# TensorE's batches 8 to 31 as a hardware loop, with fixed K and V slots, in a cached grouped-query attention block

## The chip, the cores and the metric

The kernel runs on one core of a Trainium2 chip. The metric is the device time of one execution in microseconds (us). The kernel before takes 367.31 us, the median of three runs that lie between 367.27 and 367.34.

The profile's span is about 2 us shorter than the time (365.4 against 367.2 us for the profiled run of before). Spans and stamps within a trace count from the first instruction.

## The reference, cut to what matters

```python
B, Sq, D = 32, 4, 1024
Hq, Hkv, Sk, Dh = 32, 4, 2048, 128
q = (x @ wq).reshape(B, Sq, Hq, Dh).transpose(0, 2, 1, 3)
k = jnp.repeat(k_cache, rep, axis=1)          # rep = Hq // Hkv = 8
v = jnp.repeat(v_cache, rep, axis=1)
p = softmax(einsum("bhqd,bhkd->bhqk", q, k) * Dh ** -0.5)
o = einsum("bhqk,bhkd->bhqd", p, v)
return o.transpose(0, 2, 1, 3).reshape(B, Sq, Hq * Dh) @ wo     # all bf16
```

The K and V of one batch are 2 MB each. With 32 batches and 8 MB each of wq and wo, the core must read 151 MB. That makes this a problem of keeping the DMA full (its load queue is busy 98.0% of the span, table below).

## The kernel before: the parts that matter here

Each engine has its own instruction list, written out for all 32 batches. A batch goes through these steps: VectorE transposes K (`kt`, four chunks), TensorE computes the scores (QK), VectorE the maximum, ScalarE the exponential, VectorE transposes P (`pt`), POOL spreads it into a block-diagonal operand (`pd`), TensorE multiplies by V (PV), and a small product turns O around (OT). At the end the output product uses wo.

K, V, wq and wo go through eight SBUF slots of 2 MB, used as a ring in load order. All loads are issued by SyncE (SP) in program order, and each waits until the last user of its slot is done:

```python
for n, (kind, b) in enumerate(loads):
    s = ring_slot(n)
    before, holder[s], slot_of[kind, b] = holder.get(s), (kind, b), s
    waits = [] if before is None else ["qproj"] if before == "w" else [
        ("kt", before[1], NCH - 1) if before[0] == "k" else ("pv", before[1])]
    ...
    p.dma("sp", lambda e, s=s, src=src: e.dma_start(big[:, s, :, :], src), waits, (kind, b), f"s_b{s}")
```

Every instruction that somebody waits for increments the one semaphore of its engine, and a wait compares with an absolute count:

```python
def op(self, engine, emit, waits=(), done=None):
    ...
    if done is not None:
        self.count[engine] += 1
        self.at[done] = (engine, self.count[engine])
```

From batch 9 on, one of the eight slots becomes the second buffer of the spread P (`PF_sb`); until then there are eight slots for loads.

Of the kernel before, what the change touches and what calls it, by code (L numbers as in the profile page):

```python
# [29 lines left out]
class _Program:  # L30
# [6 lines left out]
    def __init__(self):  # L37
        self.ops = {e: [] for e in self.ENGINES}
        self.count = {e: 0 for e in self.ENGINES}
        self.at = {}  # L40
        self.dma_count = {}
        self.last_pool = None

    def op(self, engine, emit, waits=(), done=None):
        if engine == "pool":
            done = done or ("pool", self.count["pool"])
            waits = tuple(waits) + (self.last_pool,) * (self.last_pool is not None)
            self.last_pool = done
        if done is not None:
            assert done not in self.at, done  # L50
            self.count[engine] += 1
            self.at[done] = (engine, self.count[engine])
        self.ops[engine].append((emit, tuple(waits), done is not None, None))

    def dma(self, engine, emit, waits, done, sem):
        assert done not in self.at, done
        self.dma_count[sem] = self.dma_count.get(sem, 0) + 16
        self.at[done] = (sem, self.dma_count[sem])
        self.ops[engine].append((emit, tuple(waits), False, sem))

    def emit(self, name, engine, sems):
        seen = {}
        for emit, waits, counted, dma_sem in self.ops[name]:
            need = {}
            for w in waits:
                s, n = self.at[w]
                if seen.get(s, 0) < n:
                    need[s] = max(need.get(s, 0), n)
            for s, n in need.items():
                engine.wait_ge(sems[s], n)  # L70
                seen[s] = n
            ins = emit(engine)
            if counted:
                ins.then_inc(sems[name], 1)
            if dma_sem is not None:
                ins.then_inc(sems[dma_sem], 16)


def bass_standalone__gqa_block_cached__sampling_kernel(
# [23 lines left out]
    SL = 17  # L103
    SW = 12
    SPB = 9
# [8 lines left out]
    with ExitStack() as es:  # L114
# [42 lines left out]
        for c in range(4):  # L157
            p.dma("sp", lambda e, c=c: e.dma_start(w_sb[:, 2 * c:2 * c + 2, :], wq_v[:, 2 * c:2 * c + 2, :]),  # L158
                  [], ("wq", c), f"s_b{c}")

        loads = [("k", b) for b in range(LEAD)]
        for b in range(B):
            ahead = [b + LEAD] if b < SL else [b + LEAD, b + LEAD + 1] if b == SL else [b + LEAD + 1]
            loads += [("k", a) for a in ahead if a < B] + [("v", b)]
        n_pd = loads.index(("k", SPB + LEAD))
        spare = (NW + n_pd) % NS
        pd_holder = loads[n_pd - NS]

        def ring_slot(n):
            if n < n_pd:  # L170
                return (NW + n) % NS
            return (spare + 1 + (n - n_pd) % (NS - 1)) % NS

        PF_sb = big[:, spare, :, :].rearrange("p t d -> p (t d)").rearrange("p (t g q w) -> p t g q w", t=T // 2, g=G, q=32)
        slot_of = {}
        holder = {s: "w" for s in range(NW)}
        for n, (kind, b) in enumerate(loads):
            s = ring_slot(n)
            before, holder[s], slot_of[kind, b] = holder.get(s), (kind, b), s
            waits = [] if before is None else ["qproj"] if before == "w" else [  # L180
                ("kt", before[1], NCH - 1) if before[0] == "k" else ("pv", before[1])]
            src = (k_cache if kind == "k" else v_cache)[b].rearrange("g (r t) d -> (g r) t d", r=R)
            p.dma("sp", lambda e, s=s, src=src: e.dma_start(big[:, s, :, :], src), waits, (kind, b), f"s_b{s}")
        n = len(loads)
        wo_slot = [ring_slot(n + c) for c in range(NW)]
# [6 lines left out]
        for c, m in enumerate(WO):  # L192
            assert h0 // 8 == (h0 + m - 1) // 8
            kind, b = holder[wo_slot[h0 // 8]]
# [17 lines left out]
        p.op("pool", lambda e: e.memset(words(PD_sb[:, :, :, :, :].rearrange("p t g q w -> p (t g q w)")), 0.0), [], "pd0")  # L212

# [47 lines left out]
        freed = [("qe", m, 1) for m in range(4)]  # L261

        def slot(free):
            n = len(freed)
            freed.append(free)
            return ring[n % 4], [freed[n - 4]]
# [4 lines left out]
        def qd(i):  # L271
            for g in range(G):
# [5 lines left out]
                     ("qd", i) if g == G - 1 else None)  # L278

        def kt(i, chunks):  # L280
            for c in chunks:
                ts = slice(TC * c, TC * (c + 1))
                src = words(big[:, slot_of["k", i], ts, :].rearrange("p t d -> p (t d)"))
                dst = words(KT_sb[:, i % 2, ts, :, :, :].rearrange("p t a r w -> p (t a r w)"))
                waits = [("k", i)] + ([("qk", i - 2)] if i > 1 else ["qt_all"] if i == 1 else [])
                p.op("dve", lambda e, s=src, d=dst: e.transpose(d, s), waits, ("kt", i, c))  # L286

        def pe_qk(i):
            waits = [("kt", i, NCH - 1), ("qd", i)] + ([("exp", i - 1)] if i else [("qs", j) for j in range(8)])
            for a in range(2):  # L290
                for w in range(2):
                    for c in range(NCH):
# [10 lines left out]
                        p.op("pe", mm, waits, ("qk", i) if last and c == NCH - 1 else None)  # L303
# [6 lines left out]
        def softmax_exp(i):  # L310
# [3 lines left out]
                [("negmx", i)] + ([("pt", i - 1)] if i else ["qproj"]), ("exp", i))  # L314

# [6 lines left out]
        def pd_of(i):  # L322
            return PF_sb if i > SPB and i % 2 else PD_sb

        def pd(i):
            free = [j for j in range(i) if pd_of(j) is pd_of(i)]
            free = ("pv", free[-1]) if free else "pd0" if pd_of(i) is PD_sb else "pf0"
            for g in range(G):
# [3 lines left out]
                p.op("pool", lambda e, s=src, d=dst: e.tensor_copy(d, s), [("pt", i), free], ("pd", i, g))  # L332

        def pe_pv(i, t):
            if t == 0:
                ring_of["o", i], waits = slot(("o", i))
# [154 lines left out]
```

## Time and profile before

| what | value |
|---|---|
| time | 367.31 us (367.27 to 367.34) |
| DMA queue 1 | busy 98.0%, 421 to 434 GB/s in slices 2 to 37 |
| TensorE / VectorE busy | 78% / 74% |
| one batch in the chain of waits | 8.92 us |
| K and V of one batch on the DMA | 2 x 4.89 us = 9.79 us |

Parts 1 to 3 of the profile page of before show busy time by engine, then the span in 40 equal slices (a digit is the busy share in tenths), then the DMA queues with packets, MB and share. In all views PE is TensorE's products, PEld its weight loads, DVE VectorE, ACT ScalarE, POOL GpSimd, and SPq the load issues of SyncE:

```profile
span 365.4 us, 6102 instructions
...
PE 285.7 (78%) x2837; PEld 140.1 (38%) x2368; DVE 271.7 (74%) x270; ACT 107.6 (29%) x135; POOL 166.9 (46%) x265
...
PEclk9998668999999999998889999999999999989999
DMA  8999999999999999999999999999999999999993
GB/s 328 430 425 429 434 429 421 430 429 428 428 429 425 427 427 426 427 430 425 430 427 427 425 424 424 421 430 429 430 429 425 427 425 423 429 423 423 406 402 120
...
q1 hardware_dynamic: 12416, 151.39, 98.0%
q8 instruction: 20, 0.33, 0.4%
```

The DMA row is full from end to end, so, apart from the 4.2 us between the last landing and the end, the kernel can only end earlier if the DMA ends earlier. Queue 8 looks negligible at 0.4%. It is not. The page lists its 20 packets as instructions; they are 16 KB each and about 1.05 us long (0.93 to 1.10). I take them for TensorE's program; at 5,261 TensorE instructions there are 20. The next table shows what they do.

Each load has 16 landings in the trace (1,296 for 81 transfers), which I read as one for each of the 16 DMA engines. The wait for a load ended with the last of them: the wo piece that closes the chain below lands from 353.84 to 358.65 us, and its wait ended at 358.65. I computed this table from the trace's landing records. For the load that lands n-th after the first piece of wq, I subtract n x 4.894 us and give the first and the last of its 16 landings.

```
kernel before       first   last
n=10   (57 us)       0.03   0.34
n=12   (67 us)       0.03   1.61
n=16   (86 us)       0.00   1.66
n=24  (126 us)      -0.01   1.79
n=67  (336 us)      -0.02   4.78
last wo piece       356.46 us / 361.19 us
```

The least disturbed engine keeps its pace to within 0.1 us for 336 us. The most disturbed one falls back in three steps of about 1.3 us (0.3 to 1.6, 1.8 to 3.1, 3.4 to 4.7), after the 1st, 9th and 17th packet of queue 8, which start at 61.6, 191.5 and 308.7 us; it ends at 4.8 us. That every eighth packet met the same engine is read from these steps: the trace does not number the engines.

The end of the chain of waits of before (start, duration, what) shows that the last wo pieces close the kernel:

```profile
295.96 25.15 DMA big<-in_v_cache_dram
...
340.31 18.34 DMA big<-in_wo_dram
```

### The profile page before, as it was taken

To read this page: it belongs to the slowest core of one execution; us is meant where nothing else is said; L and a number is where in the kernel's file an instruction comes from. 1 tells how busy PE (TensorE), PEld (TensorE's weight loads), DVE (VectorE), ACT (ScalarE), POOL (GpSimd) and SP (SyncE) were. 2 spreads that over 40 slices of the span, in tenths; PEclk is the share of its full clock that TensorE was granted. 3 is DMA by queue.
4 is the path that set the end of the run, shared out by engine and by line. 5 is a ranking of instruction groups with operands and counts; after the bars stand their busy time and mean duration, and the time that the engine had idled before them with its cause. 6 is when DMAs were issued, how large, how long until landed. Compare 5 with 4: busy or idle time off the path is not lost.

```text
span 365.4 us, 6102 instructions
## 1 busy us (share of the span) xinstructions
PE 285.7 (78%) x2837; PEld 140.1 (38%) x2368; DVE 271.7 (74%) x270; ACT 107.6 (29%) x135; POOL 166.9 (46%) x265
## 2 busy tenths in 40 slices
PE   1972666888888888877778888888888886889896
PEld 1002001444444444432234444444444443458821
DVE  0029577999999999997788999999999999854000
ACT  1010112333333373332333333333333333334100
POOL 5002150555555555753554555555555555436400
PEclk9998668999999999998889999999999999989999
DMA  8999999999999999999999999999999999999993
GB/s 328 430 425 429 434 429 421 430 429 428 428 429 425 427 427 426 427 430 425 430 427 427 425 424 424 421 430 429 430 429 425 427 425 423 429 423 423 406 402 120
DMA packets 12586, 151.90 MB, mean 416 GB/s; under 512 B 1296, under 2 KB 1552, under 8 KB 3856
## 3 DMA queue, kind: packets, MB, share of 16 engines
q1 hardware_dynamic: 12416, 151.39, 98.0%
q8 instruction: 20, 0.33, 0.4%
q10 hardware_dynamic: 144, 0.13, 0.1%
q14 instruction: 6, 0.05, 0.0%
HBM read 151.26 MB, written 0.26 MB: 415 GB/s over the span
## 4 chain that ended last, share of the span: by engine, by line
PE 37%; DVE 22%; ACT 19%; DMA 18%; issue 2%; POOL 2%; SPq 0%; POOLq 0%
PE ps_s L16 24%; ACT P_sb L311 18%; DVE mx L306 17%; PE ps_s L298 9%; DMA big<-in_v_cache_dram 7%; DMA big<-in_wq_dram 6%; DMA big<-in_wo_dram 5%; PE ps_r L341 4%; DVE KT_sb L286 2%; POOL PD_sb L332 2%; DVE negmx L307 1%; DVE QT_sb L258 1%; DVE KT_sb L242 1%; PE ps_s L374 0%; SPq L158 0%
## 5 line engine op out<-in xcount | busy, mean ns | idle before, releaser
L286 DVE STREAM_TRANSPOSE KT_sb<-big 128x1024 f32<-128x1024 f32 x128 | 150.5, 1216 | 0.8 <-DMA big<-in_k_cache_dram 0.8
L332 POOL COPY PD_sb<-PT_sb 32x1024 f32<-32x1024 f32 x84 | 86.9, 1035 | 92.0 <-PE ps_r L341 69.8
L16 PE MATMUL ps_s<-KT_sb,QD_sb 128*128 128x512 bf16 x384 | 112.3, 402 | 0.0
L311 ACT ACTIVATE P_sb<-ps_s,negmx 128x2048 bf16<-128x2048 f32 x32 | 81.4, 2545 | 96.7 <-DVE negmx L307 96.7
L298 PE MATMUL ps_s<-KT_sb,QD_sb 128*128 128x512 bf16 x128 | 51.6, 403 | 59.0 <-ACT P_sb L311 50.6
L306 DVE TENSOR_REDUCE mx<-ps_s 128x1 f32<-128x2048 f32 x32 | 73.3, 2292 | 23.5 <-PE ps_s L16 23.5
L341 PE MATMUL ps_r<-big,PD_sb 128*128 128x128 bf16 x1344 | 79.0, 219 | 2.9 <-DMA big<-in_v_cache_dram 2.2
L341 PEld LDWEIGHTS ps_r<-big,PD_sb 128*128 128x128 bf16 x1344 | 75.3, 98 | 5.7 <-DMA big<-in_v_cache_dram 2.3
L298 PEld LDWEIGHTS ps_s<-KT_sb,QD_sb 128*128 128x128 bf16 x128 | 13.0, 102 | 143.7 <-issue 78.2
L332 POOL COPY big<-PT_sb 32x1024 f32<-32x1024 f32 x44 | 45.5, 1035 | 41.0 <-PE ps_r L341 38.6
L319 DVE STREAM_TRANSPOSE PT_sb<-P_sb 128x1024 f32<-128x1024 f32 x32 | 39.9, 1245 | 14.4 <-ACT P_sb L311 14.4
L277 POOL COPY QD_sb<-QT_sb 32x64 f32<-32x64 f32 x128 | 29.5, 230 | 41.7 <-DVE QT_sb L258 25.5
L341 PE MATMUL ps_r<-big 128*128 128x128 bf16 x704 | 42.8, 223 | 3.0 <-DMA big<-in_v_cache_dram 2.4
L364 ACT ACTIVATE oT_sb<-ps_r 128x128 bf16<-128x128 f32 x32 | 8.9, 278 | 116.1 <-PE ps_r L359 116.1
L341 PEld LDWEIGHTS ps_r<-big 128*128 128x128 bf16 x704 | 40.9, 100 | 3.6 <-DMA big<-in_v_cache_dram 2.7
L382 DVE CAST P_sb<-ps_s 128x512 bf16<-128x512 f32 x1 | 0.7, 692 | 25.8 <-PE ps_s L374 25.8
L359 PEld LDWEIGHTS ps_r<-ident,o_sb 128*64 128x64 bf16 x128 | 4.6, 109 | 31.2 <-issue 29.0
L242 DVE CAST KT_sb<-ps_r 128x512 bf16<-128x512 f32 x2 | 1.3, 687 | 19.9 <-PE ps_r L226 19.9
L16 PE MATMUL ps_s<-big,oT_sb 128*128 128x512 bf16 x32 | 12.1, 379 | 0.7 <-ACT oT_sb L364 0.7
L348 ACT ACTIVATE o_sb<-ps_r,rinv 128x128 bf16<-128x128 f32 x32 | 11.2, 350 | 3.7 <-PE ps_r L341 3.7
L374 PE MATMUL ps_s<-big,oT_sb 128*128 128x512 bf16 x30 | 11.4, 379 | 0.2 <-DMA big<-in_wo_dram 0.2
L16 PE MATMUL ps_s<-big,P_sb 128*128 128x512 bf16 x32 | 9.1, 411 | 0.0
(29 smaller groups left out, 60.8 us busy)
## 6 DMA issues: line engine op xcount, KB each, us to landing
big<-in_k_cache_dram SPq DMA_DIRECT2D x32, 2048.0 KB, 21.7
big<-in_v_cache_dram SPq DMA_DIRECT2D x32, 2048.0 KB, 20.4
big<-in_wq_dram SPq DMA_DIRECT2D x4, 2048.0 KB, 13.9
big<-in_wo_dram SPq DMA_DIRECT2D x7, 1024.0 KB, 27.2
big<-in_wo_dram SPq DMA_DIRECT2D x1, 512.0 KB, 17.2
big<-in_wo_dram SPq DMA_DIRECT2D x2, 256.0 KB, 14.9
P_sb<-in_x_dram SPq DMA_DIRECT2D x1, 256.0 KB, 2.9
out_dram<-P_sb SPq DMA_DIRECT2D x1, 128.0 KB, 1.8
```

Source lines behind the costliest of these rows:

```text
L16: return eng.add_instruction(mybir.InstMatmult(name=nc.get_next_instruction_name(), engine=eng.engine, start_tensor_calc=start, stop_tenso ...
L277: p.op("pool", lambda e, s=src, d=dst: e.tensor_copy(d, s), waits if g == 0 else [], ("qd", i) if g == G - 1 else None)
L286: p.op("dve", lambda e, s=src, d=dst: e.transpose(d, s), waits, ("kt", i, c))
L298: mm = lambda e, a_=(out_, lhsT, rhs), f=first, l=last: e.matmul(a_[0], lhsT=a_[1], rhs=a_[2], start=f, stop=l, skip_group_check=True)
L306: p.op("dve", lambda e: e.tensor_reduce(mx[:, i % 4:i % 4 + 1], ps_s[:, :], AX.X, ALU.max), [("qk", i)], ("mx", i))
L311: p.op("act", lambda e: e.activation(P_sb[:, :, :, :].rearrange("p t r w -> p t w r"), ps_s[:, :].rearrange("p (t w r) -> p t w r", w=2, r=R),
L319: p.op("dve", lambda e: e.transpose(dst, src), [("exp", i)] + ([("pd", i - 2, G - 1)] if i > 1 else []), ("pt", i))
L332: p.op("pool", lambda e, s=src, d=dst: e.tensor_copy(d, s), [("pt", i), free], ("pd", i, g))
L341: p.op("pe", lambda e: e.matmul(buf[:, 0:Dh], lhsT=pd_of(i)[:, t // 2, :, :, t % 2].rearrange("p g q -> p (g q)"), rhs=big[:, slot_of["v", ...
L348: p.op("act", lambda e: e.activation(o_sb[:, :], buf[:, 0:Dh], ACT.Copy, scale=rinv[:, i % 4:i % 4 + 1]), [("pv", i), ("rinv", i)] + ([("o ...
L364: p.op("act", lambda e: e.activation(oT_sb[:, :, :, i * Sq:(i + 1) * Sq].rearrange("p h e s -> p e h s"), buf[:, 0:128].rearrange("p (e h ...
L374: mm = lambda e, a=(out_, lhsT, rhs), h=h: e.matmul(a[0], lhsT=a[1], rhs=a[2], start=(h == 0), stop=(h == Hq - 1), skip_group_check=True)
```

## The change

The intent is that TensorE's program shrinks from 5,261 instructions to 2,228, because batches 8 to 31 run as six turns of a loop over four batches. The body is written once, with the same wait values and addresses in all six turns. An absolute count, which grows from turn to turn, does not fit it, so TensorE's waits become tokens that are counted down when taken. For the addresses, V has four fixed slots (b mod 4), K has three (b mod 3), and the eighth slot is the second P buffer from the start. Idle products (4 of 512 columns per batch) are added between QK and PV from batch 4 on, with four more after PV in batches 4 to 7. PV falls back by one batch over batches 4 to 7, in the kernel before over 12 to 15. VectorE takes five of the eight copies of the last two P spreads. The order of the load queue is retuned.

The core of the diff, with cuts marked:

```diff
+    def op(self, engine, emit, waits=(), done=None, takes=(), gives=None):
+        ...
+        if gives is not None:
+            self.late[engine].append(done)
+        elif done is not None:
             self.count[engine] += 1
-            self.at[done] = (engine, self.count[engine])
+            for d in [done] + self.late[engine]:
+                self.at[d] = (engine, self.count[engine])
+            self.late[engine] = []
 ...
+        run(ops[:marks[0]])
+        with engine.Fori(0, len(parts)):
+            run(parts[0])
+        run(ops[marks[-1]:])
 ...
+            loads += [("v", b)] + ks if b < S1 else ks + [("v", b)]
+
+        def slot_of(kind, b):
+            return b % VS if kind == "v" else VS + b % KS        # VS = 4, KS = 3
 ...
-                p.op("dve", lambda e, s=src, d=dst: e.transpose(d, s), waits, ("kt", i, c))
+                p.op("dve", lambda e, s=src, d=dst: e.transpose(d, s), waits, ("kt", i, c), gives="t_kt" if c == NCH - 1 else None)
 ...
-            waits = [("kt", i, NCH - 1), ("qd", i)] + ([("exp", i - 1)] if i else [...])
+            takes = [("t_kt", 1), ("t_qd", 1)] + [("t_exp", 1)] * (i > 0)
 ...
-            return PF_sb if i > SPB and i % 2 else PD_sb
+            return PF_sb if i % 2 else PD_sb
 ...
-                p.op("pool", ..., ("pd", i, g))
+                p.op("dve" if i >= B - 2 and g < i - B + 4 else "pool", ..., ("pd", i, g))
 ...
+            if SW <= i < B:
+                pe_idle(4)
 ...
+        p.loop = starts[SW + EASE:B + 1:4]
```

In this program an instruction increments one semaphore.

More of the change, by code (lines that the diff above doesn't have):

```diff
@@ L40, in __init__ @@
         self.at = {}
+        self.late = {e: [] for e in self.ENGINES}
         self.dma_count = {}
         self.last_pool = None
-    def op(self, engine, emit, waits=(), done=None):
+        self.loop = None
+    def op(self, engine, emit, waits=(), done=None, takes=(), gives=None):
         if engine == "pool":
@@ L48, in op @@
             self.last_pool = done
-        if done is not None:
-            assert done not in self.at, done
+        if gives is not None:
+            self.late[engine].append(done)
+        elif done is not None:
             self.count[engine] += 1
-            self.at[done] = (engine, self.count[engine])
-        self.ops[engine].append((emit, tuple(waits), done is not None, None))
-    def dma(self, engine, emit, waits, done, sem):
+            for d in [done] + self.late[engine]:
+                assert d not in self.at, d
+                self.at[d] = (engine, self.count[engine])
+            self.late[engine] = []
@@ L56, in dma, with give @@
+        self.ops[engine].append((emit, tuple(waits), tuple(takes), (gives or engine, 1) if done is not None else None))
+    def give(self, engine, after, gives):
+        self.ops[engine].append((None, (after,), (), (gives, 1)))
+    def dma(self, engine, emit, waits, done, sem, taken=False):
         assert done not in self.at, done
         self.dma_count[sem] = self.dma_count.get(sem, 0) + 16
-        self.at[done] = (sem, self.dma_count[sem])
-        self.ops[engine].append((emit, tuple(waits), False, sem))
+        if not taken:
+            self.at[done] = (sem, self.dma_count[sem])
+        self.ops[engine].append((emit, tuple(waits), (), (sem, 16)))
@@ L61, in emit, with run @@
     def emit(self, name, engine, sems):
         seen = {}
-        for emit, waits, counted, dma_sem in self.ops[name]:
-            need = {}
-            for w in waits:
-                s, n = self.at[w]
-                if seen.get(s, 0) < n:
-                    need[s] = max(need.get(s, 0), n)
-            for s, n in need.items():
-                engine.wait_ge(sems[s], n)
-                seen[s] = n
-            ins = emit(engine)
-            if counted:
-                ins.then_inc(sems[name], 1)
-            if dma_sem is not None:
-                ins.then_inc(sems[dma_sem], 16)
+        def run(ops):
+            for emit, waits, takes, gives in ops:
+                need = {}
+                for w in waits:
+                    s, n = self.at[w]
+                    if seen.get(s, 0) < n or emit is None:
+                        need[s] = max(need.get(s, 0), n)
+                for s, n in need.items():
+                    ins = engine.wait_ge(sems[s], n)
+                    seen[s] = n
+                for s, n in takes:
+                    engine.wait_ge(sems[s], n).then_inc(sems[s], -n)
+                if emit is not None:
+                    ins = emit(engine)
+                if gives is not None:
+                    ins.then_inc(sems[gives[0]], gives[1])
@@ L79, in bass_standalone__gqa_block_cached__sampling_kernel @@
+        ops = self.ops[name]
+        if name != "pe":
+            return run(ops)
+        marks = self.loop
+        parts = [ops[a:b] for a, b in zip(marks, marks[1:])]
+        for part in parts:
+            assert [o[1:] for o in part] == [o[1:] for o in parts[0]] and not any(o[1] for o in part)
+        run(ops[:marks[0]])
+        with engine.Fori(0, len(parts)):
+            run(parts[0])
+        run(ops[marks[-1]:])
 def bass_standalone__gqa_block_cached__sampling_kernel(
@@ L102, in bass_standalone__gqa_block_cached__sampling_kernel @@
     LEAD = 3
-    SL = 17
-    SW = 12
-    SPB = 9
+    S1 = 12
+    S2 = 18
+    VS = 4
+    KS = 3
+    SW = 4
     EASE = 4
@@ L158, in bass_standalone__gqa_block_cached__sampling_kernel @@
             p.dma("sp", lambda e, c=c: e.dma_start(w_sb[:, 2 * c:2 * c + 2, :], wq_v[:, 2 * c:2 * c + 2, :]),
-                  [], ("wq", c), f"s_b{c}")
+                  [], ("wq", c), f"s_w{c}")
         loads = [("k", b) for b in range(LEAD)]
         for b in range(B):
-            ahead = [b + LEAD] if b < SL else [b + LEAD, b + LEAD + 1] if b == SL else [b + LEAD + 1]
-            loads += [("k", a) for a in ahead if a < B] + [("v", b)]
-        n_pd = loads.index(("k", SPB + LEAD))
-        spare = (NW + n_pd) % NS
@@ L167, in bass_standalone__gqa_block_cached__sampling_kernel @@
-        pd_holder = loads[n_pd - NS]
-        def ring_slot(n):
-            if n < n_pd:
-                return (NW + n) % NS
-            return (spare + 1 + (n - n_pd) % (NS - 1)) % NS
-        PF_sb = big[:, spare, :, :].rearrange("p t d -> p (t d)").rearrange("p (t g q w) -> p t g q w", t=T // 2, g=G, q=32)
-        slot_of = {}
-        holder = {s: "w" for s in range(NW)}
-        for n, (kind, b) in enumerate(loads):
-            s = ring_slot(n)
-            before, holder[s], slot_of[kind, b] = holder.get(s), (kind, b), s
-            waits = [] if before is None else ["qproj"] if before == "w" else [
-                ("kt", before[1], NCH - 1) if before[0] == "k" else ("pv", before[1])]
+            ahead = b + LEAD + (b >= S2)
@@ new lines, in bass_standalone__gqa_block_cached__sampling_kernel @@
+            ks = [("k", a) for a in range(len(loads) - b, ahead + 1) if a < B]
+            loads += [("v", b)] + ks if b < S1 else ks + [("v", b)]
+        def slot_of(kind, b):
+            return b % VS if kind == "v" else VS + b % KS
+        PF_sb = big[:, NS - 1, :, :].rearrange("p t d -> p (t d)").rearrange("p (t g q w) -> p t g q w", t=T // 2, g=G, q=32)
+        for kind, b in loads:
+            s = slot_of(kind, b)
+            waits = ["qproj"] * (b < VS) if kind == "v" else []
+            if kind == "v" and b >= VS:
+                waits = [("pv", b - VS)]
+            if kind == "k" and b >= KS:
+                waits = [("kt", b - KS, NCH - 1)]
@@ L182, in bass_standalone__gqa_block_cached__sampling_kernel @@
             src = (k_cache if kind == "k" else v_cache)[b].rearrange("g (r t) d -> (g r) t d", r=R)
-            p.dma("sp", lambda e, s=s, src=src: e.dma_start(big[:, s, :, :], src), waits, (kind, b), f"s_b{s}")
-        n = len(loads)
-        wo_slot = [ring_slot(n + c) for c in range(NW)]
+            p.dma("sp", lambda e, s=s, src=src: e.dma_start(big[:, s, :, :], src), waits, (kind, b), f"s_b{s}", kind == "v")
+        wo_for = [("k", B - 3), ("k", B - 2), ("k", B - 1), ("v", B - 4)]
+        wo_slot = [slot_of(kind, b) for kind, b in wo_for]
@@ L193, in bass_standalone__gqa_block_cached__sampling_kernel @@
             assert h0 // 8 == (h0 + m - 1) // 8
-            kind, b = holder[wo_slot[h0 // 8]]
+            kind, b = wo_for[h0 // 8]
             if m > 1:
@@ L212, in bass_standalone__gqa_block_cached__sampling_kernel @@
         p.op("pool", lambda e: e.memset(words(PD_sb[:, :, :, :, :].rearrange("p t g q w -> p (t g q w)")), 0.0), [], "pd0")
+        p.op("pool", lambda e: e.memset(words(PF_sb.rearrange("p t g q w -> p (t g q w)")), 0.0), [], "pf0")
         for kt in range(KT):
@@ L258, in bass_standalone__gqa_block_cached__sampling_kernel, with slot @@
                 p.op("dve", lambda e, s=src, d=dst: e.tensor_copy(d, s), [("qt", m)], ("qe", m, a))
-        freed = [("qe", m, 1) for m in range(4)]
-        def slot(free):
-            n = len(freed)
-            freed.append(free)
-            return ring[n % 4], [freed[n - 4]]
+        used = []
+        def slot():
+            used.append(len(used))
+            return ring[used[-1] % 4]
         ring_of = {}
@@ L278, in qd @@
                      ("qd", i) if g == G - 1 else None)
+            p.give("pool", ("qd", i), "t_qd")
         def kt(i, chunks):
@@ L282, in kt @@
                 ts = slice(TC * c, TC * (c + 1))
-                src = words(big[:, slot_of["k", i], ts, :].rearrange("p t d -> p (t d)"))
+                src = words(big[:, slot_of("k", i), ts, :].rearrange("p t d -> p (t d)"))
                 dst = words(KT_sb[:, i % 2, ts, :, :, :].rearrange("p t a r w -> p (t a r w)"))
                 waits = [("k", i)] + ([("qk", i - 2)] if i > 1 else ["qt_all"] if i == 1 else [])
-                p.op("dve", lambda e, s=src, d=dst: e.transpose(d, s), waits, ("kt", i, c))
+                p.op("dve", lambda e, s=src, d=dst: e.transpose(d, s), waits, ("kt", i, c), gives="t_kt" if c == NCH - 1 else None)
         def pe_qk(i):
-            waits = [("kt", i, NCH - 1), ("qd", i)] + ([("exp", i - 1)] if i else [("qs", j) for j in range(8)])
+            waits = [] if i else [("qs", j) for j in range(8)]
+            takes = [("t_kt", 1), ("t_qd", 1)] + [("t_exp", 1)] * (i > 0)
             for a in range(2):
@@ L302, in pe_qk @@
                                 nc, e, *a_, tile_size=(128, 128), tile_position=(0, 0), start=f, stop=l)
-                        p.op("pe", mm, waits, ("qk", i) if last and c == NCH - 1 else None)
+                        p.op("pe", mm, waits, ("qk", i) if last and c == NCH - 1 else None, takes)
+                        waits, takes = [], []
         def softmax_max(i):
@@ L314, in softmax_exp @@
                 [("negmx", i)] + ([("pt", i - 1)] if i else ["qproj"]), ("exp", i))
+            if i < L:
+                p.give("act", ("exp", i), "t_exp")
         def pt(i):
@@ L322, in pd_of @@
         def pd_of(i):
-            return PF_sb if i > SPB and i % 2 else PD_sb
+            return PF_sb if i % 2 else PD_sb
         def pd(i):
-            free = [j for j in range(i) if pd_of(j) is pd_of(i)]
-            free = ("pv", free[-1]) if free else "pd0" if pd_of(i) is PD_sb else "pf0"
+            free = ("pv", i - 2) if i > 1 else ("pd0", "pf0")[i]
             for g in range(G):
@@ L331, in pd @@
                 dst = words(pd_of(i)[rows, :, g, :, :].rearrange("p t q w -> p t (q w)"))
-                p.op("pool", lambda e, s=src, d=dst: e.tensor_copy(d, s), [("pt", i), free], ("pd", i, g))
+                p.op("dve" if i >= B - 2 and g < i - B + 4 else "pool", lambda e, s=src, d=dst: e.tensor_copy(d, s), [("pt", i), free], ("pd", i, g))
+            if i < B - 2:
+                p.give("pool", ("pd", i, G - 1), "t_pd")
         def pe_pv(i, t):
+            takes, waits = [], []
             if t == 0:
-                ring_of["o", i], waits = slot(("o", i))
-                waits = waits + [("pd", i, g) for g in range(G)] + [("v", i)]
-            else:
-                waits = []
+                ring_of["o", i] = slot()
+                takes = [("t_pd", 1)] * (i < B - 2) + [(f"s_b{slot_of('v', i)}", 16)]
+                waits = [] if i < B - 2 else [("pd", i, g) for g in range(G)]
             buf = ring_of["o", i]
@@ L342, in pe_pv, with pe_idle @@
                 buf[:, 0:Dh], lhsT=pd_of(i)[:, t // 2, :, :, t % 2].rearrange("p g q -> p (g q)"),
-                rhs=big[:, slot_of["v", i], t, :], start=(t == 0), stop=(t == T - 1)),
-                waits, ("pv", i) if t == T - 1 else None)
+                rhs=big[:, slot_of("v", i), t, :], start=(t == 0), stop=(t == T - 1)),
+                waits, ("pv", i) if t == T - 1 else None, takes)
+        def pe_idle(n):
+            out_, lhsT = ring[len(used) % 4], ident[:, :]
+            rhs = QT_sb[:, 0:4, :, :, :, :].rearrange("p b a h s w -> p (b a h s w)")
+            for c in range(n):
+                if c == 0:
+                    mm = lambda e: e.matmul(out_, lhsT=lhsT, rhs=rhs, start=True, stop=True, skip_group_check=True)
+                else:
+                    mm = lambda e: _matmul_held(nc, e, out_, lhsT, rhs, tile_size=(128, 128), tile_position=(0, 0), start=True, stop=True)
+                p.op("pe", mm)
         def o_evac(i):
@@ L348, in o_evac @@
             p.op("act", lambda e: e.activation(o_sb[:, :], buf[:, 0:Dh], ACT.Copy, scale=rinv[:, i % 4:i % 4 + 1]),
-                 [("pv", i), ("rinv", i)] + ([("oT", i - 1)] if i else []), ("o", i))
+                 [("pv", i), ("rinv", i)] + ([("oT", i - 1)] if i else []), ("o", i), gives="t_o")
         def pe_ot(i):
-            buf, waits = slot(("ot", i))
-            ring_of["ot", i] = buf
+            buf = ring_of["ot", i] = slot()
             for e_ in range(2):
@@ L359, in pe_ot @@
                     p.op("pe", lambda e, a=(out_, lhsT, rhs): e.matmul(a[0], lhsT=a[1], rhs=a[2], start=True, stop=True),
-                         waits + [("o", i)] if e_ == u == 0 else [], ("oT", i) if e_ == u == 1 else None)
+                         [], ("oT", i) if e_ == u == 1 else None, [("t_o", 1)] if e_ == u == 0 else [])
         def ot_evac(i):
@@ L378, in oproj @@
                             nc, e, *a, tile_size=(128, 128), tile_position=(0, 0), start=(h == 0), stop=(h == Hq - 1))
-                    p.op("pe", mm, [("wo", c), ("ot", B - 1), ("exp", B - 1)], ("op", j) if h == Hq - 1 else None)
+                    p.op("pe", mm, [("wo", c), ("ot", B - 1)], ("op", j) if h == Hq - 1 else None)
         def oproj_out():
@@ L391, in pv_until @@
             less = min(max(i - SW + 1, 0), EASE) * (T // EASE)
-            return max((i - 1) * T - less, 0)
+            return max((i - 1) * T - less, 0) if i < B else (i - 2) * T
         qd(0)
@@ L396, in bass_standalone__gqa_block_cached__sampling_kernel @@
         done = 0
-        for i in range(B + 2):
-            upto = pv_until(i) if i < B else (i - 2) * T if i == B else B * T
+        starts = []
+        for i in range(B + 3):
+            starts.append(len(p.ops["pe"]))
+            upto = pv_until(i)
             if i < L:
@@ L405, in bass_standalone__gqa_block_cached__sampling_kernel @@
             j = done // T - 1
-            if i < B and j >= 0 and j not in ot_done:
+            if j >= 0 and j not in ot_done:
                 ot_done.append(j)
-                pe_ot(j)
-                ot_evac(j)
+                if i < B:
+                    pe_ot(j)
+                    ot_evac(j)
+            if SW <= i < B:
+                pe_idle(4)
             if i < B:
                 softmax_exp(i)
-            if i == SPB:
-                p.op("act", lambda e: e.memzero(words(PF_sb.rearrange("p t g q w -> p (t g q w)"))),
-                     [("kt", pd_holder[1], NCH - 1) if pd_holder[0] == "k" else ("pv", pd_holder[1])], "pf0")
             if i < L:
@@ L421, in bass_standalone__gqa_block_cached__sampling_kernel @@
                 if k % T == T - 1:
-                    if i >= B and k // T - 1 not in ot_done:
-                        ot_done.append(k // T - 1)
+                    if i >= B:
                         pe_ot(k // T - 1)
@@ L426, in bass_standalone__gqa_block_cached__sampling_kernel @@
                     o_evac(k // T)
+            if SW <= i < SW + EASE:
+                pe_idle(4)
             done = upto
@@ L434, in bass_standalone__gqa_block_cached__sampling_kernel @@
         oproj_out()
-        names = list(p.ENGINES) + sorted({s for s in p.dma_count})
+        p.loop = starts[SW + EASE:B + 1:4]
+        names = list(p.ENGINES) + ["t_kt", "t_qd", "t_exp", "t_pd", "t_o"] + sorted({s for s in p.dma_count})
         sems = {n: es.enter_context(nc.semaphore(f"e_{n}" if n in p.ENGINES else n)) for n in names}
```

## The prediction

> **What bounds the kernel now.** DMA, throughout. The page gives DMA as 9 tenths in nearly every slice at 425 to 430 GB/s; 2 MB loads land 4.89 us apart from 8 to 336 us. No engine is as full (PE 78%, DVE 74%). In the chain of waits a batch's own cycle (QK, max, exp) repeats every 8.92 us, against 2 x 4.89 = 9.79 us for its K and V: TensorE has 0.87 us to spare per batch.
>
> **The 16 DMA engines.** In the trace's landing records a load's first and last sixteenth are 0.3 us apart until 61 us; then the spread steps to 1.6, at 192 us to 3.1, at 307 us to 4.7, and the last wo piece has its first sixteenth at 356.46 us, its last at 361.19. Each step (about 1.3 us) follows a packet of the instruction queue: 20 packets on queue 8, 16 KB each, about 1.05 us long, some 15 us apart; every eighth hits the same engine again. [...] So fetches cost the last load up to 4.5 us.
>
> **What the change does.**
> - The loop cuts TensorE's code from 5,261 to 1,034 + 670 + 524 instructions. If the 670-instruction body is kept over its six turns, 8 or 9 fetches remain, one or two per affected engine instead of three. I estimate a last spread of 1.8 to 3.1 us: 1.7 to 3.0 us gained, all at the end of the chain (wo).
> - If the body is fetched anew each turn, 20 to 25 fetches and six stalls, nothing gained. [...] A stall under 3.5 us a turn (4 x 0.87) would hide.
> - Idle products: 4 x 0.216 = 0.9 us per batch, inside TensorE's 5.3 us wait for max and exp (beside 3.75 us PV, 0.25 us O). They should prevent half-clock stretches (seven records at 0.5), which cost nothing while DMA is full.
> - [...]
> - Tail: now PV(27) waits for V until 321.1 us, then QK, max, exp, PD(30) and PD(31) on POOL (4.3 us each), PV(31); the output product runs 348.2 to 362.0 us, TensorE-bound at 0.43 us per head, just as wo lands. VectorE taking five of eight quarters frees 2 to 4 us, so the tail can follow the earlier wo. Without this the loop would gain little.
> - Load order and fixed slots: loads stay an estimated 4 to 5 us ahead of an empty queue at the start; neutral.
>
> **Sum.** Last wo near 358.5 us, then 0.4 + 0.7 + 2.8 us for products, eviction, store: span 362.2, time 364.6 us (-0.7%), range 362.6 to 368.0. Faster by over 2% (below 360) is out of reach: even the least disturbed DMA engine ends at 356.5 us. Chances: faster 0.02, same 0.93, slower 0.05.
>
> **What would show it.** Right: 8 or 9 packets on queue 8, none between first and last turn; last wo spread under 3.2 us; loads 4.89 us apart; PEclk 9 from 100 us on; the output product waiting for wo. Wrong: 20 or more packets on queue 8; holes in PE every four batches; gaps in the DMA row; a cycle over 9.8 us.
>
> **What would make it wrong.** A jump that refetches and stalls over 3.5 us; loads held behind a fixed slot so that DMA runs dry; the tail's TensorE path staying the longer one.

The 8 or 9 packets can be worked out from the trace of before: 2,228 x 20 / 5,261 = 8.5. That the body is kept over its turns, or else fetched anew with a stall at each, were two assumptions that no run had shown yet; the 2 to 4 us of the tail are my estimate.

## The result, and the profile after

In its first four runs the changed kernel took 367.24 us median (366.77 to 368.25), against 367.32 us (367.27 to 367.43) for the kernel before, run beside it. The ratio is 1.0001, 95% interval 0.9978 to 1.0024: no difference. Six further runs (the control below) gave 366.17 us median, ratio 0.9986 (0.9965 to 1.0007). Ratios here are the mean time of one kernel's fast runs over that of the other's from the same rounds, so not quite the ratio of the medians quoted. The changed kernel also spreads over more than 2 us, where the kernel before stays within a few tenths.

The same parts of the page of after:

```profile
span 364.8 us, 6484 instructions
...
PE 303.4 (83%) x2942; PEld 142.8 (39%) x2400; DVE 276.6 (76%) x275; ACT 107.6 (30%) x134; POOL 165.7 (45%) x261
...
PEclk9998668999999999999999999999999999999999
DMA  8999999999999999999999999999999999999993
GB/s 334 431 431 426 428 424 401 415 418 425 429 431 426 429 422 428 425 429 428 428 429 430 429 427 429 426 426 431 426 428 431 428 431 427 431 428 420 402 409 140
...
q1 hardware_dynamic: 12416, 151.39, 98.3%
q8 instruction: 8, 0.13, 0.1%
```

The loop does what was hoped: 8 instruction packets instead of 20, none between 140.1 and 335.0 us by their start times in the trace. The QK of batch 12, with which the second turn begins, starts at 149.4 us, so the body of 670 instructions ran its last five turns without a packet. The clock is full from 62 us to the end. The expected 2.7 us did not arrive, and the GB/s row shows where to look: slices 7 to 9 (55 to 82 us) read 401, 415 and 418, where before has 421, 430 and 429.

The chain of waits of after closes with the same load, 0.7 us earlier:

```profile
339.68 18.30 DMA big<-in_wo_dram
```

The landing table of after:

```
kernel after        first   last
n=10   (57 us)       0.02   0.59
n=12   (67 us, K5)   0.18   2.04
n=14   (77 us, K6)   0.47   3.01
n=16   (87 us, K7)   0.70   2.84
n=24  (126 us)       0.69   3.52
n=67  (337 us)       0.70   4.14
last wo piece       357.17 us / 360.50 us
```

Something new happens at K5, K6 and K7: even the least disturbed engine loses 0.7 us there, and others lose more. In the kernel before, each packet set back single engines and left the least disturbed one on pace. A delay of all 16 points to a load queue that was empty for a moment, and the DMA view agrees: from 62 to 64 us the 16 engines were busy 84% of the time in after and moved 303 GB/s, against 92% and 385 GB/s in before; from 72 to 74 us it was 377 against 451 GB/s.

SyncE's issues in the kernel after (start, duration, what) around that time:

```profile
48.66 0.33 SPq L206 DMA_DIRECT2D big<-in_k_cache_dram  x1
49.03 0.43 SPq L206 DMA_DIRECT2D big<-in_v_cache_dram  x1
59.32 0.33 SPq L206 DMA_DIRECT2D big<-in_k_cache_dram  x1
59.69 0.43 SPq L206 DMA_DIRECT2D big<-in_v_cache_dram  x1
69.79 0.33 SPq L206 DMA_DIRECT2D big<-in_k_cache_dram  x1
```

The load issued before K5 (V2, at 49.03) has its first landing at 61.93 us. K5 is issued at 59.32, so only 2.6 us remain in hand. For K6 (69.79, V3 landing first at 71.86) it is 2.1 us.

VectorE in the kernel after and in the kernel before at the same point (start, duration, line, operation):

```profile
55.34 2.36 DVE L310 STREAM_TRANSPOSE KT_sb<-big 128x1024 f32<-128x1024 f32 x2
58.05 1.25 DVE L347 STREAM_TRANSPOSE PT_sb<-P_sb 128x1024 f32<-128x1024 f32 x1 [0.34 <-ACT P_sb L337]
```

```profile
55.25 2.36 DVE L286 STREAM_TRANSPOSE KT_sb<-big 128x1024 f32<-128x1024 f32 x2
57.96 1.25 DVE L319 STREAM_TRANSPOSE PT_sb<-P_sb 128x1024 f32<-128x1024 f32 x1 [0.34 <-ACT P_sb L311]
```

And the load of before that waits for that transpose:

```profile
57.64 0.33 SPq L183 DMA_DIRECT2D big<-in_v_cache_dram  x1
```

In before, the transposes end at 57.61 us (55.25 + 2.36) and the load goes out at 57.64. In after, they end at 57.70 and K5 goes out at 59.32, when the transpose of P, which waits for the exponential, is done. That is 1.6 us later. The queue view of waits says the same in sum, naming VectorE's last line before the release:

```profile
SPq L206 <- DVE rinv L348: 201.4, 28, 10.6
```

```profile
SPq L183 <- DVE KT_sb L286: 201.8, 30, 10.6
```

(The figures are total us, times, longest; the total itself is harmless: before has 201.8 us of the same wait, and its least disturbed engine stays on pace.) The kernel before does not run dry: at 57.64 us it issues its eleventh load of the stream after wq, while the kernel after has issued eight before K5 at 59.32. It had one slot more until batch 9, and in its ring four slots freed at 27 us took four loads at once (V0, K4, V1, K5). In after, the three V slots freed with V0's stay unused, because V1 stands in the queue behind K3, which waits for its slot until 37 us.

So theory D is this: the loop gains what was predicted, and dry spells of the load queue near 62, 72 and 82 us take most of it back. Rival J: the loop's jumps, the countdown waits or the longer TensorE work (busy 303.4 us against 285.7) cost the time, and the steps in the table are a side show.

### The profile page after: what moved, and what is told of

The parts are those of the page before. It is cut to its first block, busy times and chain, and to the rows that moved or that the text cites. A ratio compares the mean times of both kernels' runs of the same rounds, so it can differ in the third digit from the quotient of the medians.

```text
span 364.8 us, 6484 instructions
## 1 busy us (share of the span) xinstructions
PE 303.4 (83%) x2942; PEld 142.8 (39%) x2400; DVE 276.6 (76%) x275; ACT 107.6 (30%) x134; POOL 165.7 (45%) x261
## 3 DMA queue, kind: packets, MB, share of 16 engines
q1 hardware_dynamic: 12416, 151.39, 98.3%
## 5 line engine op out<-in xcount | busy, mean ns | idle before, releaser
L16 PE MATMUL ps_s<-KT_sb,QD_sb 128*128 128x512 bf16 x384 | 107.9, 389 | 0.0
L359 POOL COPY PD_sb<-PT_sb 32x1024 f32<-32x1024 f32 x62 | 64.1, 1034 | 68.1 <-PE ps_r L370 46.7
L359 POOL COPY big<-PT_sb 32x1024 f32<-32x1024 f32 x61 | 63.6, 1043 | 61.1 <-PE ps_r L370 41.5
L323 PE MATMUL ps_s<-KT_sb,QD_sb 128*128 128x512 bf16 x128 | 50.0, 391 | 34.1 <-PEq L85 34.1
L370 PEld LDWEIGHTS ps_r<-big,PD_sb 128*128 128x128 bf16 x1024 | 58.4, 98 | 15.1 <-issue 13.6
L370 PEld LDWEIGHTS ps_r<-big 128*128 128x128 bf16 x1024 | 58.2, 98 | 14.2 <-issue 13.0
L370 PE MATMUL ps_r<-big 128*128 128x128 bf16 x1024 | 59.9, 219 | 4.5 <-PEq L85 4.5
L370 PE MATMUL ps_r<-big,PD_sb 128*128 128x128 bf16 x1024 | 60.1, 219 | 3.0 <-PEq L85 3.0
L323 PEld LDWEIGHTS ps_s<-KT_sb,QD_sb 128*128 128x128 bf16 x128 | 12.6, 99 | 116.5 <-issue 116.5
L16 PE MATMUL ps_r<-QT_sb,ident 128*128 128x512 bf16 x96 | 25.9, 379 | 3.2 <-issue 3.0
```

Source lines behind the costliest of these rows:

```text
L16: return eng.add_instruction(mybir.InstMatmult(name=nc.get_next_instruction_name(), engine=eng.engine, start_tensor_calc=start, stop_tenso ...
L323: mm = lambda e, a_=(out_, lhsT, rhs), f=first, l=last: e.matmul(a_[0], lhsT=a_[1], rhs=a_[2], start=f, stop=l, skip_group_check=True)
L359: p.op("dve" if i >= B - 2 and g < i - B + 4 else "pool", lambda e, s=src, d=dst: e.tensor_copy(d, s), [("pt", i), free], ("pd", i, g))
L370: p.op("pe", lambda e: e.matmul(buf[:, 0:Dh], lhsT=pd_of(i)[:, t // 2, :, :, t % 2].rearrange("p g q -> p (g q)"), rhs=big[:, slot_of("v", ...
```

## The experiments

### Control: the changed kernel again

> Control: the changed kernel once more. In its first four runs it spread from 366.8 to 368.3 us while the kernel before stayed within 0.2. Theory D (the loads run dry near 62 and 72 us and that takes back what the loop gains) expects the same spread again, ratio 0.998 to 1.003, 8 packets on the instruction queue, and a step in the landings of all 16 engines at the loads of K5 and K6. Rival J (the loop's jumps cost TensorE time that reaches the end) expects the same total but no such step in all engines.

366.17 us median (365.69 to 368.43, six runs), ratio 0.9986 (0.9965 to 1.0007). There were 8 packets on queue 8. In its profile K5 is issued at 58.73 us, and the least disturbed engine loses 0.31 us by n=16, against 0.70 in the first profile; this profiled run took 365.94 us, the first 366.77. The spread is there, and the step too, though smaller and later than expected: nothing is lost at K5, 0.07 us by K6, the rest by K7. The comparisons below use all ten runs of the changed kernel: mean 366.94 us.

The two profiles differ in when K5 is released (59.32 and 58.73 us). TensorE's clock is granted at half rate in several stretches before 62 us, together 17.0 us (34.0 to 61.3) in the first profile and 13.6 us in this one, and QK takes longer in them: one of its products takes up to 632 ns there, against 377 ns in the median (L323 of the first profile). That this is what makes the other runs vary is not shown; they have no trace.

### The loop written out

```diff
-        with engine.Fori(0, len(parts)):
-            run(parts[0])
+        for part in parts:
+            run(part)
```

> The changed kernel with its six turns written out, everything else equal (same waits, slots, idle products). Theory D: 19 to 21 packets on the instruction queue, the last wo piece with a spread of 5 to 6 us between first and last sixteenth, 369 to 370.5 us, that is 2 to 3 us slower than with the loop. Rival J: no slower, or faster by the cost of five jumps (below 367).

369.11 us median (367.42 to 371.48), ratio 1.0038 (1.0022 to 1.0054). The mean of the six runs is 369.17 us, 2.2 us above the changed kernel's 366.94. The profile shows 21 instruction packets:

```profile
q8 instruction: 21, 0.34, 0.4%
```

The last wo piece has a spread of 7.1 us (358.08 to 365.15 us), more than the 5 to 6 expected. This profiled run was the slowest of its six, and its dry spells were worse (the first landing is 1.60 us late by n=16, with K5 issued at 60.24). Rival J in the form "a jump costs time" falls: without the jumps the kernel is slower. How much of the 2.2 us is the loop cannot be read from this pair, since the dry spells differ too.

The trace agrees. From the end of the exponential (with the reading of its sum) to the first product of the next QK the changed kernel takes 0.19 us in each of the batches 1 to 26, and just as much where a jump lies between (batches 12, 16, 20 and 24). The kernel before takes 0.14.

### Releasing the K slot when the transpose ends

```diff
-                p.op("dve", ..., ("kt", i, c), gives="t_kt" if c == NCH - 1 else None)
+                p.op("dve", ..., ("kt", i, c))
+                if c == NCH - 1:
+                    p.give("dve", ("kt", i, c), "t_kt")
```

> Only the last K transpose of a batch is counted on VectorE's own semaphore again (and passed on to TensorE by a separate give), so that a K slot is free for the next load when its transpose ends and not 1.2 to 1.7 us later with VectorE's next counted instruction. Theory D: K5 is issued near 57.7 instead of 59.3 us, K6 near 68.2 instead of 69.8; the dry spells shrink to under 0.2 us; 365 to 366.3 us. Rival J: no change beyond 0.3 us.

365.52 us median (365.43 to 365.63), ratio 0.9952 (0.9939 to 0.9965). All five runs lie within 0.2 us: the unsteadiness is gone. K5 goes out at 56.62 us, K6 at 66.86. Part of that is a shorter half-clock time in this profile (13.6 us before 62 us, against 17.0); kt_early below, with 17.0 us, has K5 1.3 us earlier than the changed kernel's first profile.

```profile
56.62 0.33 SPq L206 DMA_DIRECT2D big<-in_k_cache_dram  x1
56.99 0.43 SPq L206 DMA_DIRECT2D big<-in_v_cache_dram  x1
66.86 0.33 SPq L206 DMA_DIRECT2D big<-in_k_cache_dram  x1
```

The first landing stays on pace (-0.01 at n=12, 14 and 16). The largest lag at n=67 is 3.16 us, though, more than one round of instruction packets explains. 1.0 us of it came in one step at n=63 (316 us), right after an 8 KB packet of the other instruction queue (queue 14) at 315.0 us. This edit adds 32 instructions to VectorE (the trace lists 342 instead of 310). The kt_pooltail and kt_noidle profiles below, which carry the same edit, show a step of 0.9 us at n=63 after such packets at 314.9 and 316.9 us.

### One slot more at the start

```diff
-        loads = [("k", b) for b in range(LEAD)]
+        loads = [("k", b) for b in range(LEAD + 1)]      # K3 at once, in the eighth slot
 ...
-            return PF_sb if i % 2 else PD_sb
+            return PF_sb if i % 2 and i > KS else PD_sb  # cleared after K3 is transposed
```

(The slots and waits of the K loads and the place of the clearing follow from these two lines.)

> Only the eighth slot, which the change gave to the second P buffer from the start, first holds K3 and becomes the P buffer after K3 is transposed (as in the kernel before, there from batch 9). Loads are then one deeper until batch 4. Theory D: no step in all engines at K5 and K6, last wo spread near 2 us, 364.5 to 366 us. Rival J: no change beyond 0.3 us.

A miss: 377.74 us (376.66 to 378.86), ratio 1.0279. The dry spells at K5 and K6 are gone as expected (first landing -0.02 at n=12 and 14), but my edit made a worse one. With one P buffer until batch 4, PV falls behind, the four V slots come free late, and the first landing is 12.7 us late by n=24. The GB/s row of this kernel shows the holes in slices 12 to 14:

```profile
GB/s 334 428 435 428 430 423 433 426 407 413 430 197 372 165 395 423 431 422 428 431 428 430 425 431 425 430 430 428 430 426 430 430 426 430 426 430 424 403 409 165
```

So the total says nothing about the first dry spells. It does say that the eighth slot was given to P for a reason: with V in four fixed slots, a late PV stops the loads.

### The loop alone, with the dry spells gone

This is the ktcount kernel with the loop written out (both edits above).

> The ktcount kernel (dry spells gone, 365.52 us, last wo piece spread 3.0 us) with the loop's six turns written out. This is the loop alone, with nothing else in the way. Theory F (each 16 KB instruction packet sets one DMA engine back by about 1.3 us, every eighth hits the same engine): 20 or 21 packets, last spread 4.8 to 5.8 us, 367.3 to 368.6 us, steady within 0.3 us. Rival J (a jump costs): not slower than 365.6.

367.36 us median (367.22 to 368.93), ratio 1.0013 (0.9999 to 1.0026). It is less steady than expected: one of the six runs lies above the expected range, two just below. There are 21 packets, and the last wo piece spreads over 4.8 us (356.39 to 361.18), as in the kernel before. By n=67 the largest lag is 4.80 us against 3.16 with the loop. The mean is 367.73 us, 2.2 us above ktcount (1.8 us by the medians). That the first pair gave 2.2 us as well is partly chance, since its dry spells differed. This confirms the first half of theory D: the loop is worth about 2 us, inside the predicted 1.7 to 3.0.

### The last P copies all on POOL

```diff
-                p.op("dve" if i >= B - 2 and g < i - B + 4 else "pool", ...
+                p.op("pool", ...
```

> The ktcount kernel with the last two P products' copies all on the POOL engine, as before. My prediction held that the loop gains little without VectorE's share. If so: the output product starts over 2 us later and the time rises by 1 us or more. The other theory, from the trace of the changed kernel: the output product there waits for wo in any case and has about 2 us in hand, so the copies on POOL cost at most 0.3 us (365.4 to 365.9).

366.45 us median (365.50 to 366.55), ratio 0.9976 (0.9963 to 0.9988). Four of the five runs are 0.9 to 1.0 us slower than ktcount's median. The fifth, the profiled one, is not (365.50 us), and its output product starts at 346.12 us, as ktcount's does at 346.10. So both expectations miss. VectorE's share is worth something near 0.9 us in most runs, but no trace of a slow run exists that would show how. This stays open. It is not what the missing 2 us hang on.

### Without the idle products

```diff
-                pe_idle(4)
+                pass                                     # both places
```

> The ktcount kernel without the idle products. If the half-clock stretches cost nothing while the loads are the limit: half clock comes back in one or several stretches after 100 us, time within 0.4 us of 365.5. If the idle products are what keeps the tail short: 1 us or more slower, with half clock near the last batches.

366.88 us median (365.77 to 368.59), ratio 0.9993 (0.9971 to 1.0015), on the ktcount kernel: 1.4 us slower by the medians and unsteady again. Half clock comes back at 95.2 and 115.7 us, 3.4 us each (a third stretch, at 320.5 us, stands in ktcount's profile too, at 319.2), and after the second one the queue runs dry:

```profile
PEclk9998788999898999999999999999999999989999
...
GB/s 325 432 432 426 430 428 428 430 421 430 428 430 426 403 412 430 430 431 430 426 428 431 427 426 430 428 428 430 423 430 432 428 428 429 427 426 424 403 409 141
```

A V load that goes out at 120.60 us in ktcount goes out at 124.03 here, and the first landing is 0.4 us late by n=25 and 0.8 by n=27. With fixed V slots a slow PV delays the next V load, so the idle products do protect the loads. The profiled run (366.23 us) is one of the three faster of the six; the slower three, 367.5 to 368.6 us, have no trace.

### The release only where it matters

```diff
-                if c == NCH - 1:
+                late = c == NCH - 1 and i >= 9           # gives t_kt itself, as in the changed kernel
+                if c == NCH - 1 and not late:
                     p.give("dve", ("kt", i, c), "t_kt")
```

> As ktcount, but the separate give only for batches 0 to 8, where the loads have no depth in hand; later batches give straight from the transpose as in the changed kernel. VectorE has 321 instructions instead of 344, so that its extra instruction page near 315 us, which came with a step of 1 us on one DMA engine, should go. Expect no dry spell, last spread near 2.0 to 2.3 us, 364.5 to 365.2 us. If the step at 315 us has another cause: 365.5.

364.82 us median (364.77 to 364.93), ratio 0.9931 (0.9919 to 0.9944). This is the loop at its predicted worth. The jumps, the countdown waits and TensorE's longer work are all still in it, so rival J falls in its other forms too. K5 goes out at 57.98 us with 3.9 us in hand (V2 lands first at 61.84). There are 8 packets on queue 8. There is no packet of queue 14 near 315 us and no step there. The last wo piece spreads over 2.24 us and lands at 358.64 us.

### The same cure by the load order alone

V1 to V5 are issued one place earlier (V0, V1, K3, V2, K4, V3, K5, ...). The late release stays.

```diff
-            ks = [("k", a) for a in range(len(loads) - b, ahead + 1) if a < B]
-            loads += [("v", b)] + ks if b < S1 else ks + [("v", b)]
+            nk, nv = (sum(kind == w for kind, _ in loads) for w in "kv")
+            ks = [("k", a) for a in range(nk, ahead + 1) if a < B]
+            vs = [("v", a) for a in range(nv, b + 1 + (b <= VS))]
+            loads += vs + ks if b < S1 else ks + vs
```

> The changed kernel with one edit in the order of the load queue: V1 to V5 are issued one place earlier (V0, V1, K3, V2, K4, V3, K5, ...), since their slots are free from 27 us on and only stand behind a K that waits for its slot. The late release of the K slots stays as it is, no instruction is added. Theory D: one more load is in hand at 59, 69 and 79 us, so the step in all 16 engines goes although K5 is still issued near 59 us; last spread 2.0 to 2.6 us; 364.7 to 365.4 us, steady within 0.3 us. If it were the late release itself that costs (TensorE or VectorE held up by it), and not the queue running dry: 366 to 368 us as before.

364.99 us median (364.84 to 366.64), ratio 0.9944 (0.9930 to 0.9959). In the profiled run K5 is issued at 60.24 us, later than in any profile of the changed kernel itself, and nothing is lost at K5, K6 or K7 (first landing 0.01 us late at each; in this order they are n=13, 15 and 17), because V3 stands before it in the queue. So it is the depth of the queue that matters, not the late release as such. The expected steadiness is a miss: two of the six runs are slower (365.66 and 366.64 us). Both had a lower mean clock (0.966 against 0.976 to 0.981), and the profile of the first shows a new step of 0.3 us in all engines between n=17 and n=23. The reorder shifts the thin place more than it removes it.

### A version that beats both

> As kt_early (364.82 us), and the last pieces of wo cut smaller: 4,4,4,4,4,4,2,2,2,1,1 heads instead of ending 4,2,1,1. In kt_early TensorE works without a pause from the landing of the last four-head piece to the end, 3.7 us. With smaller pieces it should end about 0.5 us after the last landing: 364.1 to 364.5 us. If the end is bound by the last landing alone: 364.8.

kt_early with smaller last pieces of wo:

```diff
-    WO = (4, 4, 4, 4, 4, 4, 4, 2, 1, 1)
+    WO = (4, 4, 4, 4, 4, 4, 2, 2, 2, 1, 1)
```

364.39 us median (364.20 to 364.68), ratio 0.9921 (0.9908 to 0.9934), 3.0 us below the kernel before by the medians. The last landing is where kt_early has it (358.68 against 358.64 us), and the span after it is 0.4 us shorter.

> best with the load order of vearly as well. Both cure the same dry spell, so together no faster than best by more than 0.2 us: 363.9 to 364.5 us. If each cured a different loss: 363.5 us or less.

best with the order of vearly as well: 364.28 us (364.24 to 364.86), the same ratio 0.9921. As expected, two cures of one dry spell do not add up.

### What the dry spells depended on

Time in hand is the first landing of the load before K5, minus K5's issue. Loss is how late the least disturbed engine is at K5 (n=12), K6 (n=14) and K7 (n=16).

```
profile        K5 issued  in hand   loss at K5   K6     K7
ktcount          56.62     5.2 us     -0.01    -0.01  -0.01
kt_early         57.98     3.9        -0.01     0.00  -0.02
after, control   58.73     3.2        -0.02     0.07   0.31
after, first     59.32     2.6         0.18     0.47   0.70
unrolled         60.24     1.8         0.45     1.61   1.60
```

At K5, 3.2 us in hand lost nothing, 2.6 us lost 0.18 and 1.8 us lost 0.45. The line is not sharp: K7 lost another 0.22 us with 3.2 us in hand in the first profile and 0.15 with 3.6 in the control, while K8 in vearly lost nothing with 2.4 us and K7 in k3slot 0.02 with 1.8. So some 3 us is an estimate from these profiles, and less is a risk of running dry, not a certainty.

## Why the prediction was wrong, point by point

- **DMA bounds the kernel; instruction packets delay single DMA engines.** Right. With the dry spells gone, writing the loop out costs 2.2 us by the means (1.8 by the medians) and brings back a spread of 4.8 us.
- **The body is kept over its six turns, 8 or 9 packets remain, 1.7 to 3.0 us gained.** Right: 8 packets, none from 140 to 335 us, the last five turns included, 2.2 us.
- **"Load order and fixed slots: loads stay an estimated 4 to 5 us ahead of an empty queue at the start; neutral."** This is the step that failed. K5 and K6 had 2.6 and 2.1 us in hand in the first profile, and the queue ran dry: all 16 engines lost at least 0.4 us by K6 and 0.7 us by K7. I had named "loads held behind a fixed slot so that DMA runs dry" as a way to be wrong, but set its cost at zero. I had worked out the issue times as if a K slot were still released at the end of its transpose; from the trace of before that comes to an estimated 4.4 us for K5 (K2's transposes done at 57.61 us, the load ahead of K5 due at about 62.02, where the n=11 load of before lands first). I had seen the `late` list in the diff but did not see that it moves the release to VectorE's next counted instruction, 1.6 us later. Curing it in batches 0 to 8 alone took the mean of the changed kernel from 366.94 to 364.83 us: the term I set at zero was 2.1 us. Between the two profiles the last landing differs by 1.9 us (360.50 and 358.64); 0.8 us of it is common to all engines (first landing 357.17 and 356.40), 1.1 us a wider spread (3.33 and 2.24). That the wider spread comes of the dry spells, too, is argued: by n=16 the most disturbed engine was 0.9 us later than in kt_early (2.84 and 1.97), but further steps followed near 110 and 335 us, where instruction packets start.
- **The last wo spread of 1.8 to 3.1 us and the sum of 364.6 us.** In the changed kernel's profile the spread was 3.33 us. In kt_early, without dry spells, it was 2.24 us and the time 364.82 us. The rest of the sum held. That the first median, 367.24 us, still lies in my range of 362.6 to 368.0 us is owed to the width of the range: the gain of 2.7 us was not there.
- **Idle products "should prevent half-clock stretches".** Mostly right: the changed kernel's first profile shows none from 61 us to the end, and without the idle products two come back, at 95.2 and 115.7 us. ktcount has one at 319.2 us all the same.
- **Half-clock stretches "cost nothing while DMA is full".** So it looks in the kernel before: with half clock at 167, 178 and 188 us its first landing stays on pace (-0.01 us at n=40). With fixed V slots it is not: without the idle products one stretch at 115.7 us led to a loss of 0.8 us in all engines, and the median rose by 1.4 us.
- **Waits and gives.** They added 0.05 us per batch (0.19 instead of 0.14 us from exponential to QK). That is hidden: from QK to QK a batch takes 8.98 us in the changed kernel (mean of batches 10 to 26), its loads 9.79.
- **"Without this the loop would gain little" (VectorE's share of the last P).** Too strong. The output product of the changed kernel starts at 345.8 us, that of before at 348.2, but that is not shown to come from VectorE's share: in the kt_pooltail profile, without it, the start is 346.12 us. With all copies on POOL the ktcount kernel lost 0.9 us in four runs of five and nothing in one, while the loop's 2.2 us stayed.
- **Out of reach below 360 us.** Right: the best version still takes 364.3 us, and its least disturbed DMA engine ends at 356.4 us.

## What to carry to other kernels

In this kernel, bound by DMA throughout, two things cost time: a load queue that emptied (2.1 us, changed kernel against kt_early) and single DMA engines that fell behind (2.2 us, kt_unrolled against ktcount). In a kernel like it, look at the first and last landing of each load: the busy share of the load queue, 98.0% before and 98.3% after, hardly tells the two apart. When a change gives an instruction's one signal to another waiter, follow what happens to everybody who waited on it before, above all the loads that wait for a buffer. Work out the time in hand at the shallowest point of the load queue (here 2.6 us at K5 and 2.1 us at K6), not in the steady state.
